# Query tiles loaded twice from DRAM and scaled while scores are copied, in a threshold-attention and mixture-of-attention kernel

## The chip, the cores and the metric

The kernel runs on one core of one Trainium2 chip. The metric is the device time of one execution in microseconds (us). Three executions of the kernel before took 933.61, 934.09 and 937.35 us; their median, 934.09 us, is the time before. TensorE is called PE here (its weight loads PEld), VectorE DVE, ScalarE ACT, GpSimd POOL, and the engine that only issues transfers SP.

## The reference, cut to what matters

Eight batches, eight heads, 576 positions, head size 64. The first part is an attention whose scores below the row's maximum minus `tau` are dropped; its output, with heads side by side, is the input of the second part, four causal attentions ("experts") of which a gate takes the best two at each position.

```python
scale = 1.0 / np.sqrt(q.shape[-1])                     # 1/8
scores = scale * np.matmul(q, k.transpose(0, 1, 3, 2))
thresh = np.max(scores, axis=-1, keepdims=True) - tau
scores = np.where(scores >= thresh, scores, -1000000000.0)
attn = np.exp(scores - np.max(scores, axis=-1, keepdims=True))
attn = attn / (np.sum(attn, axis=-1, keepdims=True) + 1e-09)
x = np.matmul(attn, v)                                 # then (8, 576, 512)
logits = x @ w_gate                                    # best 2 of 4 experts
for e in range(4):
    q, k, v = x @ wq[e], x @ wk[e], x @ wv[e]
    a = softmax(causal(scale * (q @ k.transpose(0, 2, 1))))
    out += weight[e] * (a @ v @ wo[e])
```

## The kernel before, in words

**Tiling.** The first part works on 32 pairs of heads: pair n is batch n // 4 and heads 2 (n % 4) and the next. A head's 576 queries are four tiles of 128 rows and a tail of 64; the two tails of a pair make one tile. A score tile is 128 rows by 576 keys and fills two banks of PSUM. So a pair has nine score tiles, and the program 288. PE holds float32 operands as two parts, a rounded one (`hi`) and the rest (`lo`), and makes each product from three matmuls; much of it runs on one half of the array, two matmuls side by side.

**A pair, step by step.** `load(n)` (line 365) sends the transfers: eight of keys (`ki`), two of queries (`qi`), two of query tails (`qit`), three of values (`vm`, `vt`). `scale_q` and `scale_qt` (lines 871 to 875) multiply the queries by `qsc`, which is minus 1/8, and write them twice side by side (`qi2`, `qit2`): on POOL for every pair but the first, which has them on ACT and DVE. `prep(n)` (line 391) turns keys and queries round on PE, ACT writes the `hi` part (`kk`, `qq`, `qz`) and DVE the `lo` part. `scores` (line 408) then does, for each tile: the matmuls (`s_main`, line 932); `s_min` on DVE (line 945), which copies the scores out of PSUM with an addition of zero and keeps the row's minimum (the sign is turned, so that is the maximum's place); `s_thr`, the threshold; `s_exp` on ACT (line 960); `s_stt`, the mask (line 962), a DVE instruction that reads scores and exponentials from SBUF, compares, multiplies and sums; `tr_pp`, transposes of the result on PE (profile line 826); and `out_t`, their copy to SBUF on ACT (line 812, out of `ps` into `pt`). `attnv` (line 448) sums the row sums, inverts them, spreads them with POOL into `iw` (lines 977 to 983), transposes them on PE and multiplies by `v` (`av`).

**The second part**, `second(b)` (line 515), projects the whole batch with PE, evacuates each result with an ACT copy and a DVE addition, runs the gate, scores, exponentials, POOL scaling (`p`, line 1225), transposes, products and output. It starts when the four pairs of a batch are done and is mixed with the pairs of the next batch. The last batch's second part has no pairs beside it.

**What sets the order.** The kernel makes a list of tasks, and `plan` (line 155) runs an event simulation over them when the program is built: each task has a length per engine, a priority, buffers that it takes (`SLOTS`) and tasks that it waits for. An idle engine takes the ready task of least priority. The priorities are sums of the table `PR`, the rates `PJ`, `VJ`, `S2J`, `TAILK`, and some hundreds of numbers in `TUNE`. Engines then execute their own lists strictly in the order planned. Until `COLD`, PE fills its gaps with matmuls on a constant tile (`ones`).

**Queues.** Transfers are issued by SP or by ACT; an issue stands in the engine's list with its other work. `load` sets `e = "SP" if n else "ACT"` for the queries, and so they are planned. The transfers are lambdas that read `e` when they are called, and line 380 has set `e` to "POOL" or "DVE" by then; `dma` (line 838) sends everything that is not "SP" to ACT. Thus all 128 query transfers are issued by ACT, at the places where the plan had SP issue them. Transfers of both queues take turns on eight completion semaphores, `DMAHW0` to `DMAHW7`; an issue that takes one of them again waits until the transfer that had it before is complete.

Of the kernel before, what the change touches and what calls it, by code (L numbers as in the profile page):

```python
# [11 lines left out]
F32 = mybir.dt.float32  # L12
# [72 lines left out]
class Space:  # L85
# [8 lines left out]
    def pick(self, cls, now, taken, kept):  # L94
        ok = [self.banks[i] <= now and i not in taken and i not in kept and (i != IDLE or now >= COLD) for i in range(8)]
        if cls == "s":
            pairs = [i for i in range(0, 6 if now <= EARLY else SHI, 2) if ok[i] and ok[i + 1]]
            return pairs[0] if pairs and sum(ok) - 2 >= LEAVE else None
        if cls == "d":
            pairs = [i for i in range(DLOW, 8, 2) if ok[i] and ok[i + 1]]  # L100
            return pairs[-1] if pairs else None
# [53 lines left out]
def plan(tasks, filler=None):  # L155
# [9 lines left out]
    moved = 0.0  # L165
# [11 lines left out]
    def begin(e, now):  # L177
        best, full, kept = None, set(), set()
        for pri, _, t in ready[e]:
# [3 lines left out]
            if e == "PE":  # L183
# [4 lines left out]
                if best is not None and p >= best[0]:  # L188
                    continue
# [13 lines left out]
    while events:  # L203
# [23 lines left out]
        for e in engines:  # L227
# [24 lines left out]
            at[e], t.end = start + occ, start + lat  # L252
# [11 lines left out]
def t_act(n):  # L264
    return 172 + 0.84 * n, 110
# [29 lines left out]
def work(K):  # L295
# [69 lines left out]
    def load(n):  # L365
        b, hp = divmod(n, NPAIR)
        pri = 5 * (n - 1) - 3.0 + PR["ld"]
        ki, qi, qit, qi2, qit2, vm = (Buf(x) for x in ("ki", "qi", "qit", "qi2", "qit2", "vm"))
# [3 lines left out]
        dq = [dma(lambda j=j: K.load_q(n, j, e), (), pri + 0.01, [qi], name=f"ldq.{n}", e=e) for j in range(2)]  # L372
        dt = [dma(lambda j=j: K.load_qt(n, j, e), (), pri + 0.01, [qit], move=72.0, name=f"ldq.{n}", e=e) for j in range(2)]
# [17 lines left out]
    def prep(n):  # L391
        ki, qi, qit, vm, dk, sq, st, dv = LD[n]
# [925 lines left out]
```

## Time and profile before

| | |
|---|---|
| median of three executions | 934.09 us |
| the profiled execution | 935.23 us, of which the span from the first to the last instruction 933.3 us |
| busy, share of the span | PE 95%, PEld 84%, DVE 79%, ACT 75%, POOL 46% |
| mean granted PE clock | 0.995 of full speed |

A share of busy time is a mean over the whole span. An engine that is not busy was waiting for another, or it was issuing a transfer, which isn't counted as busy. The chain of waits starts at the last instruction and goes back, at each step to what released it; it says which engine's work was last at each moment, and its shares add up to the span. PE can be busy with other work while the chain runs over ACT or DVE.

### The profile page before, as it was taken

How to read it: one execution, taken by the hardware profiler on the slowest of the kernel's cores; microseconds unless marked ns; L12 is line 12 of the kernel's file. 1: busy time of each engine (PE TensorE's matmuls, PEld its weight loads, DVE VectorE, ACT ScalarE, POOL GpSimd, SP SyncE). 2: the span in 40 equal slices, each digit the busy share in tenths (PEclk: the TensorE clock that was granted, in tenths of full speed). 3: DMA queues.
4: the chain of work that ended last, by engine and by line, in shares of the span. 5: the costliest groups of instructions: out<-in, count | busy, mean ns of one | idle time of the engine just before them, and what ended most of it. 6: DMA issues, size and time to landing. Idle time of an engine off the chain costs nothing.

```text
span 933.3 us, 36267 instructions
## 1 busy us (share of the span) xinstructions
PE 882.3 (95%) x14809; PEld 785.9 (84%) x14809; DVE 740.0 (79%) x2114; ACT 700.8 (75%) x1491; POOL 428.7 (46%) x724
## 2 busy tenths in 40 slices
PE   9888999999999999989999899998999999999997
PEld 7777898889887998879888798877988789887996
DVE  5899898777888768896888968798787977888554
ACT  5888869776787767887777876887677886778546
POOL 4654344632644436345265433644335533453373
PEclk9999999999999999999999999999999999999999
DMA  3433111120111202112111211112021121110001
GB/s 78 103 82 73 32 39 41 40 63 25 40 41 40 63 21 56 41 40 51 31 50 36 59 45 53 36 34 69 17 61 42 42 59 27 40 26 2 25 25 58
DMA packets 131030, 42.21 MB, mean 45 GB/s; under 512 B 126000, under 2 KB 126000, under 8 KB 130864
## 3 DMA queue, kind: packets, MB, share of 16 engines
q1 hardware_dynamic: 91808, 30.44, 12.9%
q10 hardware_dynamic: 39056, 9.45, 4.6%
q8 instruction: 117, 1.92, 0.9%
q14 instruction: 49, 0.40, 0.1%
HBM read 30.42 MB, written 9.44 MB: 43 GB/s over the span
## 4 chain that ended last, share of the span: by engine, by line
PE 58%; DVE 16%; ACT 10%; POOL 6%; issue 5%; DMA 3%; ACTq 1%; POOLq 0%; DVEq 0%
PE ps L836 46%; PE ps L826 12%; DVE e L964 6%; ACT pt L812 5%; DVE sc L947 4%; DMA vm<-in_v_dram 3%; ACT e L960 2%; POOL p L1225 2%; ACT p L1205 2%; DVE sm L1198 1%; ACTq L839 1%; POOL q2d L816 1%; POOL k L820 1%; DVE iv L1027 1%; DVE qq L820 1%
## 5 line engine op out<-in xcount | busy, mean ns | idle before, releaser
L812 ACT ACTIVATE pt<-ps 128x640 f32<-128x640 f32 (+3 forms) x400 | 251.6, 661 | 50.7 <-PE ps L826 43.2
L964 DVE SCALAR_TENSOR_TENSOR e<-sc,sm,e 128x576 f32<-128x576 f32 x288 | 250.3, 884 | 28.0 <-ACT e L960 24.6
L960 ACT ACTIVATE e<-sc,sm 128x576 f32<-128x576 f32 x288 | 220.7, 774 | 52.1 <-DVE sc L947 32.6
L947 DVE TENSOR_SCALAR_CACHE_REDUCE sc<-ps 128x576 f32<-128x576 f32 x288 | 215.2, 751 | 47.0 <-PE ps L836 42.8
L836 PE MATMUL ps<-kk,qq 64*128 64x288 f32 x1536 | 173.9, 325 | 6.0 <-ACT pt L812 3.1
L836 PE MATMUL ps<-pt,vm 128*64 128x128 f32 (+1 forms) x2560 | 159.9, 267 | 0.2
L826 PE MATMUL ps<-ident,e 64*128 64x64 f32 x2880 | 139.5, 228 | 13.7 <-ACT pt L812 4.6
L1225 POOL TENSOR_SCALAR p<-p,sm,gw 128x384 f32<-128x384 f32 (+4 forms) x144 | 100.9, 708 | 108.3 <-ACT pt L812 34.2
L826 PEld LDWEIGHTS ps<-ident,e 64*128 64x128 f32 x2880 | 118.6, 139 | 29.9 <-ACT pt L812 9.9
L836 PEld LDWEIGHTS ps<-pt,vm 128*64 128x64 f32 x2560 | 128.8, 137 | 11.9 <-issue 4.2
L836 PEld LDWEIGHTS ps<-kk,qq 64*128 64x128 f32 x1536 | 119.7, 191 | 20.1 <-ACT pt L812 7.2
L836 PE MATMUL ps<-x,wh 64*128 64x288 f32 x1024 | 105.0, 294 | 0.0
L816 POOL TENSOR_SCALAR iw<-sg 128x256 f32<-128x256 f32 (+1 forms) x96 | 44.5, 475 | 101.7 <-DVE sg L972 64.2
L836 PEld LDWEIGHTS ps<-x,wh 64*128 64x128 f32 x1024 | 87.3, 185 | 0.5 <-ACT pt L812 0.3
L836 PE MATMUL ps<-x,wl 64*128 64x288 f32 x512 | 81.5, 292 | 0.0
L812 ACT ACTIVATE iv<-ps 128x288 f32<-128x288 f32 (+2 forms) x128 | 53.0, 422 | 34.5 <-PE ps L836 19.5
L1205 ACT ACTIVATE p<-ps,sm 128x512 f32<-128x512 f32 (+3 forms) x128 | 67.2, 531 | 10.2 <-DVE sm L1198 9.7
L836 PE MATMUL ps<-pt,v 128*64 128x128 f32 (+1 forms) x960 | 60.9, 264 | 7.1 <-DVE sc L947 3.9
L836 PE MATMUL ps<-wh,x 64*128 64x260 f32 x640 | 66.2, 286 | 0.0
L869 POOL TENSOR_SCALAR qi<-qi,qsc 128x1024 f32<-128x1024 f32 x31 | 38.0, 1224 | 52.6 <-PE ps L826 50.8
L836 PE MATMUL ps<-pt,vt 128*64 128x128 f32 (+1 forms) x640 | 59.1, 262 | 0.0
L836 PEld LDWEIGHTS ps<-pt,v 128*64 128x64 f32 x960 | 45.3, 138 | 15.9 <-DVE sc L947 6.8
(124 smaller groups left out, 1631.0 us busy)
## 6 DMA issues: line engine op xcount, KB each, us to landing
ki<-in_k_dram SPq DMA_DIRECT2D x256, 36.0 KB, 1.9
qi<-in_q_dram ACTq DMA_DIRECT2D x64, 128.0 KB, 2.7
vm<-in_v_dram SPq DMA_DIRECT2D x64, 128.0 KB, 2.6
out_dram<-ob SPq DMA_DIRECT2D x32, 256.0 KB, 2.1
qit<-in_q_dram ACTq DMA_DIRECT2D x64, 16.0 KB, 2.0
vt<-in_v_dram SPq DMA_DIRECT2D x32, 32.0 KB, 2.4
out_dram<-ob SPq DMA_DIRECT2D x8, 128.0 KB, 2.4
ob<-in_moe_wq_dram SPq DMA_DIRECT2D x4, 128.0 KB, 2.4
```

The source lines that it names most:

```text
L812: self.nc.scalar.activation(dst, src, AF.Copy)
L816: self.nc.gpsimd.tensor_scalar(dst, src, 1.0, 0.0, op0=ALU.mult, op1=ALU.add)
L820: eng.tensor_tensor(dst, a, b.bitcast(F32), op=ALU.subtract)
L826: self.nc.tensor.transpose(self.ps[:, bank, c * n:(c + 1) * n], x[sl], self.ident[sl, sl])
L836: self.nc.tensor.matmul(out, x, y, start=first, stop=last)
L839: (self.nc.sync if e == "SP" else self.nc.scalar).dma_start(dst, src)
L869: (self.nc.vector if e == "DVE" else self.nc.gpsimd).tensor_scalar(out, t, self.qsc, 0.0, op0=ALU.mult, op1=ALU.add)
L947: self.nc.vector.tensor_scalar(self.sides(sc), self.dbank(s)[:, :, :HS], 0.0, None, op0=ALU.add, op1=ALU.min, accum_out=self.small(sm)[:, ...
L960: self.nc.scalar.activation(self.row(e), self.row(sc), AF.Exp, bias=self.small(sm)[:, 2 * j:2 * j + 1], scale=-1.0)
L964: self.nc.vector.scalar_tensor_tensor(self.row(e), self.row(sc), self.small(sm)[:, 8 + j:9 + j], self.row(e), op0=ALU.is_le, op1=ALU.mult, ...
L1205: self.nc.scalar.activation(self.p2(p2)[:, j * SM:j * SM + w], self.dbank(g)[:, j, :w], AF.Exp, bias=m[:, 2 * j:2 * j + 1], accum_out=m[:, ...
L1225: self.nc.gpsimd.tensor_scalar(p, p, self.small(sm)[:, 10 + j:11 + j], g[:, o:o + 1], op0=ALU.mult, op1=ALU.mult)
```

## The change

Queries go straight into `qi2` and `qit2`: each transfer is sent twice, once for each of the two copies. The scaling steps are gone; `s_min` multiplies by `qsc` in the place where it added zero. The buffers `qi` and `qit` fall away, `e` gets a sixth and `q2d` a second buffer. The lambdas now read an `e` that isn't set again, so pairs 1 to 31 issue their queries from SP and pair 0 from ACT. `plan` learns that the mask waits for POOL and POOL for the mask (`port`); pairs of PSUM banks may start at an odd number (`ODD`); the spreading of `iw` may go to POOL or ACT (`IWE`). The lengths that `plan` takes for `s_min`, `s_exp`, `s_stt` and ACT's small step, six constants, the tile order of the first batch (`TS0`) and every number of `TUNE` are new.

```diff
-    "qi": 1, "ki": 1, "qit": 1, "qi2": 1, "qit2": 1, "vm": 2, "kk": 2, "qq": 2, "qz": 2, "sc": 4, "e": 5, "sg": 3, "iw": 1, "iv": 3, "pt": 8,
-    "x0": 2, "x1": 2, "x2": 1, "x3": 1, "sm": 8, "q2": 2, "k2": 2, "q2d": 1, "p2": 3, "v2": 2,
+    "ki": 1, "qi2": 1, "qit2": 1, "vm": 2, "kk": 2, "qq": 2, "qz": 2, "sc": 4, "e": 6, "sg": 3, "iw": 1, "iv": 3, "pt": 8,
+    "x0": 2, "x1": 2, "x2": 1, "x3": 1, "sm": 8, "q2": 2, "k2": 2, "q2d": 2, "p2": 3, "v2": 2,
...
+            elif t.port:
+                p += SHY * max(0.0, at["POOL"] - now - 200.0)
...
-            at[e], t.end = start + occ, start + lat
+            more = 0.0
+            if t.port:
+                more = max(0.0, at["POOL"] - start - 200.0)
+                port = start + more + 640.0
+            elif e == "POOL":
+                more = max(0.0, port - start)
+            at[e], t.end = start + occ + more, start + lat + more
...
-        dq = [dma(lambda j=j: K.load_q(n, j, e), (), pri + 0.01, [qi], name=f"ldq.{n}", e=e) for j in range(2)]
-        dt = [dma(lambda j=j: K.load_qt(n, j, e), (), pri + 0.01, [qit], move=72.0, name=f"ldq.{n}", e=e) for j in range(2)]
+        dq = [dma(lambda j=j, x=x: K.load_q(n, j, x, e), (), pri + 0.01, [qi2], name=f"ldq.{n}", e=e) for j in range(2) for x in range(2)]
+        dt = [dma(lambda j=j, x=x: K.load_qt(n, j, x, e), (), pri + 0.01, [qit2], move=72.0, name=f"ldq.{n}", e=e) for j in range(2) for x in range(2)]
...
-        e = "POOL" if n else "DVE"
-        st = task(e, (270, 30), lambda: K.scale_qt(e), dt, 5 * (n - 1) - 1, [qit2], [qit], name=f"qs.{n}")
-        e2 = "POOL" if n else "ACT"
-        sq = task(e2, (1200, 30) if n else t_act(2 * SM), lambda: K.scale_q(e2), dq, 5 * (n - 1) - 1, [qi2], [qi], name=f"qs.{n}")
-        LD[n] = (ki, qi2, qit2, vm, dk, sq, st, dv)
+        LD[n] = (ki, qi2, qit2, vm, dk, dq, dt, dv)
...
-            m = task("DVE", (825, 75), lambda j=j: K.s_min(bufs[j], scs[j], sm, j), [a], i + PR["max"], [],
+            m = task("DVE", (747, 75), lambda j=j: K.s_min(bufs[j], scs[j], sm, j), [a], i + PR["max"], [],
...
-        u = [task("POOL", t_pool(nm * P), lambda: K.g_wide(sg, iw, nm), [r], i + PR["nrm"], [iw], [sg, iw], name=f"iw.{n}.{first}")]
+        u = [evac(nm * P, lambda e: K.g_wide(e, sg, iw, nm), [r], i + PR["nrm"], [iw], [sg, iw], name=f"iw.{n}.{first}", engs=IWE)]
...
+IWE = ('POOL', 'ACT')
...
-W_FROM = 23858.152
-W_EACH = 2325.47
+W_FROM = 19276.174
+W_EACH = 6514.406
...
-        self.nc.vector.tensor_scalar(self.sides(sc), self.dbank(s)[:, :, :HS], 0.0, None, op0=ALU.add, op1=ALU.min,
+        self.nc.vector.tensor_scalar(self.sides(sc), self.dbank(s)[:, :, :HS], self.qsc, None, op0=ALU.mult, op1=ALU.min,
```

**Where it moves instructions.** On ACT, in the middle of the program, at the place where pair 20's queries have been turned and pair 22's are sent for. Before (`qq`, `pt`, `e`, `p` are the tiles of the steps above):

```order
L812 ACTIVATE qq_838_10378<-ps 128x512
L812 ACTIVATE pt_840_10417<-ps 128x640
L839 DMA qi<-in_q_dram 128x4x64 x2
L812 ACTIVATE pt_842_10439<-ps 128x512
L960 ACTIVATE e_844_10462<-sc_841_10429,sm_83 128x576
L812 ACTIVATE pt_845_10475<-ps 128x640
L812 ACTIVATE pt_846_10486<-ps 128x640
L812 ACTIVATE pt_848_10493<-ps 128x512
L839 DMA qit<-in_q_dram 64x64
L960 ACTIVATE e_849_10502<-sc_843_10449,sm_83 128x576
L839 DMA qit<-in_q_dram 64x64
```

The same place of ACT's list now:

```order
L828 ACTIVATE qq_837_10398<-ps 128x512
L828 ACTIVATE pt_839_10439<-ps 128x640
L828 ACTIVATE pt_840_10461<-ps 128x512
L828 ACTIVATE pt_841_10481<-ps 128x512
L828 ACTIVATE pt_842_10494<-ps 128x640
L828 ACTIVATE pt_844_10506<-ps 128x640
L963 ACTIVATE e_846_10527<-sc_843_10496,sm_81 128x576
```

The four issues are gone from between the copies; behind the opening, ACT's list has no transfer. The copies stand in nearly the order they had.

On SP, a little over one round of four pairs, in the middle of the program. Before (`ki` keys, `vm` and `vt` values, `ob` results going out):

```order
L839 DMA ki<-in_k_dram 48x3x64 x16
L839 DMA vm_110<-in_v_dram 128x4x64 x2
L839 DMA vt_113<-in_v_dram 64x2x64
L839 DMA ki<-in_k_dram 48x3x64 x8
L839 DMA vm_109<-in_v_dram 128x4x64 x2
L839 DMA vt_111<-in_v_dram 64x2x64
L839 DMA ki<-in_k_dram 48x3x64 x8
L839 DMA out_dram<-ob_687_8479 128x512
```

SP in the matching round now (`qi_72` and `qit_73` are the doubled buffers `qi2` and `qit2`):

```order
L855 DMA qit_73<-in_q_dram 64x64 x4
L855 DMA ki<-in_k_dram 48x3x64 x10
L855 DMA qi_72<-in_q_dram 128x4x64 x4
L855 DMA vm_108<-in_v_dram 128x4x64 x2
L855 DMA vt_111<-in_v_dram 64x2x64
L855 DMA qit_73<-in_q_dram 64x64 x4
L855 DMA qi_72<-in_q_dram 128x4x64 x4
L855 DMA ki<-in_k_dram 48x3x64 x8
L855 DMA out_dram<-ob_689_8538 128x512
```

Where a pair had 11 loads in SP's list it has 19, and the eight of the queries stand between those of the keys and the values.

At the opening of the program, on ACT. Before:

```order
L839 DMA qi<-in_q_dram 128x4x64 x2
L839 DMA qit<-in_q_dram 64x64 x2
L779 ACT_TABLE_LOAD
L779 ACTIVATE warm<-eps 128x2
L867 ACTIVATE qi_74<-qi,qsc 128x1024
L812 ACTIVATE qq_1_243<-ps 128x512 x2
```

And now:

```order
L855 DMA qi_72<-in_q_dram 128x4x64 x4
L855 DMA qit_73<-in_q_dram 64x64 x4
L828 ACT_TABLE_LOAD
L828 ACTIVATE qq_1_232<-ps 128x512
L795 ACTIVATE warm<-eps 128x2
```

Eight issues stand ahead of ACT's first instruction where there were four, and the scaling between them and `qq` is gone.

## Rows read from the trace of the kernel before

**Rows 1.** The page's first part: busy us of each engine (share of the span) x instructions.

```profile
span 933.3 us, 36267 instructions
...
PE 882.3 (95%) x14809; PEld 785.9 (84%) x14809; DVE 740.0 (79%) x2114; ACT 700.8 (75%) x1491; POOL 428.7 (46%) x724
```

**Rows 2.** Busy time in stretches of the span: the first batch of pairs, one of the middle rounds, the end; then ten-microsecond pieces of the first batch. Columns: from:to, length, busy us (x instructions) of each engine, granted PE clock, DMA share, GB/s.

```profile
0.00:128.50 128.50, 116.61 (x1847) 102.11 (x1849) 106.05 (x293) 96.79 (x177) 64.36 (x143) 0.99 0.31 69
466.90:580.00 113.10, 108.12 (x1850) 96.99 (x1848) 92.00 (x267) 86.67 (x185) 51.49 (x80) 1.00 0.19 45
868.00:933.40 65.40, 59.84 (x914) 52.80 (x910) 30.17 (x85) 36.66 (x107) 30.00 (x55) 0.99 0.11 38
40.00:50.00 10.00, 8.72 (x148) 7.37 (x148) 9.95 (x28) 9.03 (x17) 7.29 (x9) 1.00 0.48 107
50.00:60.00 10.00, 8.72 (x162) 7.22 (x156) 9.90 (x25) 8.83 (x19) 5.28 (x7) 1.00 0.45 107
```

**Rows 3.** The page's fourth part, the chain that ended last, its shares of the span by engine and by line.

```profile
PE 58%; DVE 16%; ACT 10%; POOL 6%; issue 5%; DMA 3%; ACTq 1%; POOLq 0%; DVEq 0%
PE ps L836 46%; PE ps L826 12%; DVE e L964 6%; ACT pt L812 5%; DVE sc L947 4%; DMA vm<-in_v_dram 3%; ACT e L960 2%; POOL p L1225 2%; ACT p L1205 2%; DVE sm L1198 1%; ACTq L839 1%; POOL q2d L816 1%; POOL k L820 1%; DVE iv L1027 1%; DVE qq L820 1%
```

**Rows 4.** The timeline around ACT's issues for the next pair, in the place of the first order above: start, length, engine, line, operation, and in brackets the idle time before and what ended it.

```profile
517.84 0.94 SPq L839 DMA_DIRECT2D vm<-in_v_dram  x2
518.02 1.12 POOL L869 TENSOR_SCALAR qi<-qi,qsc 128x1024 f32<-128x1024 f32 x1
...
518.72 0.71 ACT L812 ACTIVATE pt<-ps 128x640 f32<-128x640 f32 x1 [0.64 <-PE ps L826]
...
519.17 1.12 ACTq L839 DMA_DIRECT2D qi<-in_q_dram  x2
...
520.40 0.60 ACT L812 ACTIVATE pt<-ps 128x512 f32<-128x512 f32 x1 [0.97 <-DMA vm<-in_v_dram]
...
521.05 0.53 PE L826 MATMUL ps<-ident,e 64*128 64x64 f32 x10 [0.59 <-ACT pt L812]
...
522.31 0.28 PE L826 MATMUL ps<-ident,qit 64*128 64x64 f32 x2 [0.28 <-ACT pt L812]
...
522.90 0.66 PE L836 MATMUL ps<-kk,qq 64*128 64x288 f32 x6 [0.32 <-ACT pt L812]
```

**Rows 5.** The transfers' line: issues on each queue, and their length in ns, least, median and most.

```profile
L839 SPq DMA_DIRECT2D ki<-in_k_dram x256: 311/427/1835, 0.8 to 819.0; - x128
L839 ACTq DMA_DIRECT2D qi<-in_q_dram x64: 369/375/1301, 1.3 to 758.5; - x64
L839 ACTq DMA_DIRECT2D qit<-in_q_dram x64: 472/483/1317, 2.3 to 770.1; - x64
L839 SPq DMA_DIRECT2D vm<-in_v_dram x64: 372/455/1348, 5.7 to 835.5; - x64
L839 SPq DMA_DIRECT2D vt<-in_v_dram x32: 607/610/1664, 6.8 to 836.1; - x32
```

**Rows 6.** The longest waits of PE, summed over the span: who, for whom, us in total, times, longest.

```profile
PE ps L826 <- ACT pt L812: 7.7, 17, 0.7
PE ps L836 <- ACT pt L812: 6.0, 21, 0.6
PE ps L826 <- POOL iw L816: 5.7, 7, 1.1
```

**Rows 7.** Groups of POOL by shape: busy us, mean ns | idle before, releasers.

```profile
L869 POOL TENSOR_SCALAR qi<-qi,qsc 128x1024 f32<-128x1024 f32 x31 | 38.0, 1224 | 52.6 <-PE ps L826 50.8 <-DMA qi<-in_q_dram 1.8
...
L869 POOL TENSOR_SCALAR qit<-qit,qsc 128x128 f32<-128x128 f32 x31 | 15.9, 514 | 64.1 <-PE ps L826 42.1 <-DMA qit<-in_q_dram 12.0 <-DVE sm L1000 10.0
L816 POOL TENSOR_SCALAR iw<-sg 128x128 f32<-128x128 f32 x32 | 15.5, 485 | 0.0
```

**Rows 8.** The mask and the score copy: groups of DVE by shape, and the mask's lengths in ns (least, median, most).

```profile
L964 DVE SCALAR_TENSOR_TENSOR e<-sc,sm,e 128x576 f32<-128x576 f32 x288 | 250.3, 884 | 28.0 <-ACT e L960 24.6 <-ACT sm L955 1.4
L947 DVE TENSOR_SCALAR_CACHE_REDUCE sc<-ps 128x576 f32<-128x576 f32 x288 | 215.2, 751 | 47.0 <-PE ps L836 42.8 <-ACT pt L812 2.7
...
L964 DVE SCALAR_TENSOR_TENSOR e<-sc,sm,e x288: 773/817/1586, 16.9 to 866.8; 128x576 f32<-128x576 f32 x144
```

**Rows 9.** The opening, on ACT and PE.

```profile
2.30 1.50 ACTq L839 DMA_DIRECT2D qit<-in_q_dram  x2
3.83 1.28 ACT L779 ACT_TABLE_LOAD   x1 [3.83 <-DMA ki<-in_k_dram]
...
5.28 1.15 ACT L867 ACTIVATE qi<-qi,qsc 128x1024 f32<-128x1024 f32 x1
7.30 1.08 ACT L812 ACTIVATE qq<-ps 128x512 fp32r<-128x512 f32 x2 [0.87 <-PE ps L826]
...
12.05 0.60 PE L836 MATMUL ps<-kk,qq 64*128 64x288 f32 x1
```

**Rows 10.** DMA: the page's third part for the queue of the loads, the landing of queries, and the shortest round of the key buffer, from its release by PE to its next use.

```profile
q1 hardware_dynamic: 91808, 30.44, 12.9%
...
qi<-in_q_dram ACTq DMA_DIRECT2D x64, 128.0 KB, 2.7
...
588.91 0.60 PE L826 MATMUL ps<-ident,ki 48*128 48x48 f32 x11
599.44 0.69 PE L826 MATMUL ps<-ident,ki 48*128 48x48 f32 x12
```

More of the change, by code (lines that the diff above doesn't have):

```diff
@@ L66, in __init__ @@
         self.move = 0.0
+        self.port = False
         self.takes = takes
@@ L96, in pick @@
         if cls == "s":
-            pairs = [i for i in range(0, 6 if now <= EARLY else SHI, 2) if ok[i] and ok[i + 1]]
+            hi = 6 if now <= EARLY else SHI
+            pairs = [i for k in range(1 + ODD) for i in range(k, hi - k, 2) if ok[i] and ok[i + 1]]
             return pairs[0] if pairs and sum(ok) - 2 >= LEAVE else None
         if cls == "d":
-            pairs = [i for i in range(DLOW, 8, 2) if ok[i] and ok[i + 1]]
-            return pairs[-1] if pairs else None
+            pairs = [i for k in range(1 + ODD) for i in range(6 - k, DLOW - 1, -2) if ok[i] and ok[i + 1]]
+            return pairs[0] if pairs else None
         one = [i for i in range(GLOW, 8) if ok[i]]
@@ L164, in plan @@
     mode = None
-    moved = 0.0
+    moved = port = 0.0
     order = []
@@ L187, in begin @@
                     p += BACK * space.scores
[L188 to L189 removed]
+            elif t.port:
+                p += SHY * max(0.0, at["POOL"] - now - 200.0)
+            if best is not None and p >= best[0]:
+                continue
             new = [b for b in t.takes if b.slot is None]
@@ L341, in small @@
     def small(engs, fn, deps, pri, sm, name):
-        x = task(None, {e: (200, 30) if e == "POOL" else SMALL for e in engs}, None, deps, pri, [], [sm], name=name)
+        x = task(None, {e: (200, 30) if e == "POOL" else (290, 110) if e == "ACT" else SMALL for e in engs}, None, deps, pri, [], [sm], name=name)
         x.fn = lambda: fn(x.by)
@@ L367, in load @@
         pri = 5 * (n - 1) - 3.0 + PR["ld"]
-        ki, qi, qit, qi2, qit2, vm = (Buf(x) for x in ("ki", "qi", "qit", "qi2", "qit2", "vm"))
+        ki, qi2, qit2, vm = (Buf(x) for x in ("ki", "qi2", "qit2", "vm"))
         e = "SP" if n else "ACT"
@@ L472, in attnv @@
         a = None
-        for s in order:
+        if AVM:
+            a = pe(sum(10 * (109.2 if s < R else 58.4) for s in order),
+                   lambda: [K.av(g, (s - first) * P, vm, PTS[n, s][0], s) for s in order],
+                   [*LD[n][7], *[y for s in order for y in PTS[n, s][1]]], i + PR["av"], [g, x],
+                   [vm, *[y for s in order for y in PTS[n, s][0]]], "C", 53.0, name=f"av.{n}.{first}")
+        for s in order if not AVM else ():
             pts, c = PTS[n, s]
@@ L861, in load_vt @@
         self.dma(self.vts[vm.slot][ST:], self.v[b, 2 * hp:2 * hp + 2, SM:, :].rearrange("h s d -> s h d"))
-    def scaled(self, e, out, t):
-        t = t.unsqueeze(2).to_broadcast(out.shape)
-        if e == "ACT":
-            self.nc.scalar.activation(out, t, AF.Copy, scale=self.qsc)
-        else:
-            (self.nc.vector if e == "DVE" else self.nc.gpsimd).tensor_scalar(out, t, self.qsc, 0.0, op0=ALU.mult, op1=ALU.add)
-    def scale_qt(self, e):
-        self.scaled(e, self.qit2.unsqueeze(1), self.qit.unsqueeze(1))
-    def scale_q(self, e):
-        self.scaled(e, self.qi2, self.qi.rearrange("p r j d -> p (r j) d"))
     def tr_k(self, g):
```

54 lines of the change are left out of this document (29 added, 25 removed).

## The prediction

> **What bounds the kernel now.** I read the busy shares first: PE is at work for 882.3 of 933.3 us, so it idles for 51.0 us, and no other engine passes 79% [rows 1]. Then the stretches. The first batch of pairs idles PE for 128.5 - 116.6 = 11.9 us, a middle round for 113.1 - 108.1 = 5.0 us, the end for 65.4 - 59.8 = 5.6 us [rows 2]. In the first batch DVE is the bound for a while: 9.95 and 9.90 of 10 us between 40 and 60 us, while PE has 8.7 [rows 2]. The granted clock is 0.99 or more of the 2.4 GHz level in all these stretches, so the clock is not the matter.
>
> Next the chain. PE has only 58% of it; DVE has 16%, ACT 10%, POOL 6%, and 3% stands under a DMA whose line is that of the values, 1% under ACT's sequencer at line 839, a transfer's issue [rows 3]. No copy on ACT reads values from DRAM. What this means is seen in the timeline around 519 us [rows 4]: ACT has to issue two query loads; the first needs the scaled tile's source buffer, on which POOL works from 518.02 to 519.14, and the other takes a completion semaphore that SP's value loads, issued from 517.84, had before. The next copy starts at 520.40, after 0.97 us without work, and PE then waits 0.59, 0.28 and 0.32 us for ACT's copies. So a query load on ACT holds the copies queued behind it, and PE behind them. The issue alone is 375 ns for `qi` and 483 ns for `qit`, 64 of each [rows 5]: 64 x 0.375 + 64 x 0.483 = 54.9 us of ACT's list.
>
> **The change part by part.** The sum is made against the profiled execution: 935.2 us, that is 933.3 of span and 1.9 around it, 1.1 above the median.
>
> *Query loads leave ACT.* 120 of 128 issues go, near 120 x 0.43 = 52 us of ACT's list, with the waits in front of them. From above, the end moves by all that the chain has under "DMA" and "ACTq", 3% + 1% of 933 or 37 us [rows 3]; from below by nothing, if PE's queue hides it. What PE shows is nearer the low end: its waits for ACT's copies are 7.7 + 6.0 = 13.7 us [rows 6], and the one place looked at gives 0.59 + 0.28 + 0.32 = 1.2 us [rows 4]. I take 1.2 us there and 0.3 us at the other three pairs of a round together, for seven rounds: 1.5 x 7 = 10 us. What is late next there is the score copy on DVE and the exponential behind it, which have 4% and 2% of the chain. Against this, 36 of the 96 `iw` steps now stand in ACT's list; this trace has none on ACT, so I bound one from POOL's 485 ns for it [rows 7]: at most 17 us, a third of what ACT gets back.
>
> *The scaling leaves POOL.* 38.0 + 15.9 = 53.9 us of 428.7 [rows 1, 7]. POOL idles for more than half of the span, so this counts only where PE waits for POOL: 5.7 us for `iw`, in seven places [rows 6]. I take 3 us, between 0 and 5.7; DVE's row sums, from which `iw` is made, are late next.
>
> *The mask and the port.* The mask takes 884 ns in the mean, 817 in the median [rows 8]. So 288 x 0.067 = 19 us of DVE go to some long ones. POOL loses 54 of 429 us, an eighth, and the plan now sees the collision. DVE counts only where it is the bound, about a third of the first batch: I take 1 us, between 0 and 19 x 128.5 / 933 = 2.7. The Trainium skill, "SBUF — State Buffer", section "Who interferes with whom", says that a VectorE instruction with two SBUF inputs and a GpSimd instruction that reads SBUF lock each other out for the whole of an instruction. That fits long masks beside short ones in these rows. By that rule alone an estimate with random meetings would give 38.0 / 933 of the 288 masks, 12 of them, half a scaling step each, 7 us of DVE in the whole span; the sum above would get 1 us more.
>
> *The score copy multiplies.* Same engine, same shape, 288 times at 751 ns [rows 8]. The mask also reads a column of numbers per partition and costs 66 ns more with two inputs from SBUF, so the ends are 0 and 288 x 0.066 = 19 us of DVE. Nearest is the copy itself, which only changes its operation: 0.
>
> *The opening.* Eight issues stand ahead of ACT's table load where four did. Two `qit` took 1.50 us together with the waits for semaphores, and the table load started at 3.83 us [rows 9]. Four more at 0.4 to 0.75 us put it at 5.5 to 6.8; with its 1.28 us the first `qq` copy can start at 6.8 to 8.1, against 7.30. The last `qit` lands 2 to 2.7 us after its issue, near 9, and PE's list has the tails' transposes ahead of the keys', so the first score matmul comes at 12 to 14 us against 12.05. I take 1 us later, between 1 earlier (the 1.15 us of scaling are gone) and 2 later.
>
> *Twice the query bytes, on one queue.* 64 x 512 packets more for the tiles, and 4096 for the tails, 36,864 on top of 91,808 that took 12.9% of the DMA engines' time [rows 10]: 5% more, hidden by engines that are idle for over 80% of a middle round [rows 2]. SP's list has per pair 8 x 0.427 + 4 x 0.375 + 4 x 0.483 + 2 x 0.455 + 0.607 = 8.4 us of issues [rows 5] against 28 us that a pair takes, a quarter of a round [rows 2]. The cover is smallest where a key buffer is free at 589.5 and wanted again at 599.4 us [rows 10]: up to sixteen issues, 6.9 us, and 2.7 us to land are 9.6 of 9.9 us. I take 0, between 0 and 16 (2 us in each of eight rounds).
>
> *The new order.* Row counts and the sequence of copies in ACT's list are close to those before, so I give it 0, between 10 us lost and 10 won, a fifth of PE's idle time each way.
>
> Sum: - 10 - 3 - 1 + 0 + 1 + 0 + 0 = - 13 us. 935.2 - 13 = 922.2 for a profiled execution, and 1.1 less, **921 us**, as a median.
>
> **The rivals.** *PE has it hidden already.* The bound is 95% busy and its idle time has many small causes; each hold that goes uncovers the next wait, here DVE's. For it: DVE's chain share of 16% is larger than ACT's. Against it: the hold at 519 us is of ACT's own making. It would give 932 to 936, say 934 us.
>
> *Late loads.* Before, queries had a landing buffer of their own and could be two pairs ahead; now each load waits until PE has turned the pair before, and 19 loads stand in one list with the results' stores. If an issue waits for such a store, or a semaphore, for 0.7 us past the 0.3 us of cover that I find, keys and queries are late for that pair. It decides from the point where sixteen issues and a landing exceed 9.9 us; at 0.7 us in each of 31 pairs it costs 22 us, and the end is at 921 + 22 = 943 us, slower than before. For it: single key loads have taken up to 1.8 us to issue [rows 5]. Against it: SP is idle for most of a round, and the plan now counts these loads where they stand.
>
> *More than the idle time.* Weight loads are at work for 785.9 us, 84% [rows 1], and PE has only 58% of the chain [rows 3], so a matmul marked busy can be one that waits. The Trainium skill, "Perfetto Trace Analysis", section "Identifying the Most-Contended Engine", says that the busy share of matmuls measures badly how near TensorE is to its limit, and the busy share of weight loads better. In numbers of this kernel: if the chain's 37 us for DMA and ACT's sequencer go wholly, with 3 us of POOL, less 11 us that `iw` and the opening take, the end is at 934 - 29 = 905 us.
>
> **How the numbers follow.** The forecast, 912 to 929 us, has 0.56; more than the idle time 0.18; hidden already 0.14; late loads, or an order that is worse by itself, 0.12. About 0.5%, 4.7 us, is what a measurement of this kernel can tell from no change. Forecast and third rival are faster, 0.74; the first rival is the same, 0.14; the second slower, 0.12. The range reaches down to the third rival's 905 and up to 938, where it takes in the first rival and the smaller half of the second's prices; I leave some 0.08 below and 0.08 above.
>
> **What would show it.** In the page of the changed kernel no query load stands under ACT's queue except eight, and the lines "DMA" and "ACTq" of the chain fall from 4% to under 1%. PE's waits for `pt` copies fall from 13.7 to under 8 us, those for `iw` from 5.7 to under 3. POOL's busy time falls to near 360 us, the mask's mean to 840 to 870 ns, and a middle round lasts about 111 us. The score copy stays at 751 ns. I am wrong if ACT's waits shrink and the rounds stay at 113 us (hidden), if PE's transposes of keys or queries wait for a DMA (late loads), or if the score copy grows past 770 ns.

## The result: 906.25 us, 3.1% faster

Run beside each other, the kernel before took 935.43 us (median, 933.61 to 937.35) and the changed one 906.25 us (905.23 to 906.58): a ratio of 0.969, interval 0.966 to 0.971, or 29.2 us less. The forecast was 13 us less. The time is inside the predicted range, at its low end, and next to what the rival "more than the idle time" gives. The experiments below show that neither the forecast's terms nor that rival's mechanism made most of it: 19.5 of the 29 us came with the new order and what was planned along with it, and the prediction had put the order at 0. That the time lies in the range and near that rival is chance.

**The profile after.** The changed kernel's page, busy us of each engine (answering [rows 1]):

```profile
span 904.6 us, 36394 instructions
...
PE 877.8 (97%) x14813; PEld 786.4 (87%) x14813; DVE 732.3 (81%) x2106; ACT 705.5 (78%) x1533; POOL 355.4 (39%) x627
```

PE idles 904.6 - 877.8 = 26.8 us, where it idled 51.0. That is 24.2 us; the other 4.5 us of the span's 28.7 came out of PE's *busy* time, for the same matmuls. So busy time was no floor. POOL has lost 73.3 us: 53.9 are the scaling, and most of the rest are the `iw` steps that ACT has now.

Stretches of the changed kernel's span: the first batch, a middle round and the end (columns as in [rows 2]):

```profile
0.00:124.70 124.70, 113.75 (x1785) 98.87 (x1787) 103.55 (x285) 94.10 (x178) 52.04 (x128) 0.97 0.40 88
311.20:418.50 107.30, 105.93 (x1838) 95.72 (x1836) 90.30 (x264) 86.97 (x191) 41.52 (x67) 1.00 0.24 56
839.20:904.60 65.40, 60.38 (x904) 52.93 (x900) 29.70 (x85) 35.37 (x103) 28.59 (x53) 0.99 0.11 38
```

A middle round takes 107.3 us instead of 113.1, and PE idles 1.4 us of it instead of 5.0. The first batch is 3.8 us shorter, of which 0.9 are idle time (11.0 us instead of 11.9), at a granted clock of 0.97 against 0.99; the end is as long as it was. So most of the gain is in the middle.

What PE waits for in the changed kernel (us in total, times, longest; answering [rows 6]):

```profile
PE ps L842 <- DVE e L967: 3.5, 3, 2.3
PE ps L842 <- DVE sc L950: 2.4, 7, 0.8
PE ps L852 <- ACT pt L828: 2.2, 8, 0.5
...
PE ps L842 <- ACT pt L828: 0.9, 1, 0.9
...
PE ps L842 <- ACT iw L828: 0.3, 2, 0.2
```

The waits for `pt` copies are 2.2 + 0.9 = 3.1 us (13.7 before), those for `iw` 0.3 (5.7 before), and none that is listed is for a DMA. Groups by shape, for the mask and the copy (answering [rows 8]):

```profile
L967 DVE SCALAR_TENSOR_TENSOR e<-sc,sm,e 128x576 f32<-128x576 f32 x288 | 236.6, 834 | 9.1 <-ACT e L963 6.7 <-ACT sm L958 0.4
L950 DVE TENSOR_SCALAR_CACHE_REDUCE sc<-ps,qsc 128x576 f32<-128x576 f32 x288 | 232.2, 811 | 45.3 <-PE ps L852 32.5 <-PE ps L842 5.8 <-issue 3.3
```

The mask is 50 ns shorter (884 to 834), 14.4 us of DVE in all. The score copy is 60 ns *longer* (751 to 811), 17.3 us, which the prediction put at 0. Transfers: SP issues 124 of each kind of query load, ACT the eight of the opening; the queues of SP (q1) and of ACT (q10), answering [rows 5, 10]:

```profile
L855 SPq DMA_DIRECT2D qi<-in_q_dram x124: 366/497/1589, 8.8 to 774.5; - x124
L855 SPq DMA_DIRECT2D qit<-in_q_dram x124: 465/587/1774, 11.3 to 789.9; - x124
```

```profile
q1 hardware_dynamic: 167200, 48.74, 22.5%
...
q10 hardware_dynamic: 2576, 0.59, 0.3%
```

The chain of the changed kernel's profile breaks off after about a fifth of the span, so its shares can't be set beside [rows 3].

### The profile page after: what moved, and what is told of

It reads as the page before. It is cut to its first block, busy times and chain, and to the rows that moved or that the text cites. A ratio compares the mean times of both kernels' runs of the same rounds, so it can differ in the third digit from the quotient of the medians.

```text
span 904.6 us, 36394 instructions
## 1 busy us (share of the span) xinstructions
PE 877.8 (97%) x14813; PEld 786.4 (87%) x14813; DVE 732.3 (81%) x2106; ACT 705.5 (78%) x1533; POOL 355.4 (39%) x627
## 5 line engine op out<-in xcount | busy, mean ns | idle before, releaser
L950 DVE TENSOR_SCALAR_CACHE_REDUCE sc<-ps,qsc 128x576 f32<-128x576 f32 x288 | 232.2, 811 | 45.3 <-PE ps L852 32.5
L967 DVE SCALAR_TENSOR_TENSOR e<-sc,sm,e 128x576 f32<-128x576 f32 x288 | 236.6, 834 | 9.1 <-ACT e L963 6.7
L852 PE MATMUL ps<-kk,qq 64*128 64x288 f32 x1536 | 169.3, 321 | 2.8 <-DVE sc L950 1.2
L1228 POOL TENSOR_SCALAR p<-p,sm,gw 128x512 f32<-128x512 f32 (+4 forms) x144 | 101.4, 713 | 164.2 <-ACT pt L828 63.8
L842 PEld LDWEIGHTS ps<-ident,e 64*128 64x128 f32 x2880 | 122.8, 139 | 22.9 <-ACT pt L828 5.8
L852 PEld LDWEIGHTS ps<-kk,qq 64*128 64x128 f32 x1536 | 118.9, 189 | 14.4 <-DVE sc L950 3.3
L832 POOL TENSOR_SCALAR x<-iv 128x320 fp32r<-128x320 f32 (+1 forms) x64 | 37.1, 579 | 119.7 <-DVE iv L1030 61.7
L1208 ACT ACTIVATE p<-ps,sm 128x384 f32<-128x384 f32 (+3 forms) x128 | 66.3, 524 | 9.2 <-DVE sm L1201 4.2
L832 POOL TENSOR_SCALAR iw<-sg 128x256 f32<-128x256 f32 (+1 forms) x60 | 25.5, 429 | 120.7 <-DVE sg L975 65.6
L1201 DVE TENSOR_REDUCE sm<-ps 128x2 f32<-128x1024 f32 (+3 forms) x64 | 52.4, 819 | 8.6 <-PE ps L852 8.4
L852 PE MATMUL ps<-pt,v 128*64 128x128 f32 (+1 forms) x960 | 57.9, 260 | 0.2 <-DVE ob L1108 0.2
```

Of the source, the lines that this page charges most:

```text
L832: self.nc.gpsimd.tensor_scalar(dst, src, 1.0, 0.0, op0=ALU.mult, op1=ALU.add)
L842: self.nc.tensor.transpose(self.ps[:, bank, c * n:(c + 1) * n], x[sl], self.ident[sl, sl])
L852: self.nc.tensor.matmul(out, x, y, start=first, stop=last)
L950: self.nc.vector.tensor_scalar(self.sides(sc), self.dbank(s)[:, :, :HS], self.qsc, None, op0=ALU.mult, op1=ALU.min, accum_out=self.small(s ...
L967: self.nc.vector.scalar_tensor_tensor(self.row(e), self.row(sc), self.small(sm)[:, 8 + j:9 + j], self.row(e), op0=ALU.is_le, op1=ALU.mult, ...
L1201: self.nc.vector.tensor_reduce(self.small(sm)[:, :3:2], self.dbank(g)[:, :, :w], axis=AX.X, op=ALU.max, negate=True)
```

## The experiments

Times are medians; the kernel before took 935.2 to 935.6 us beside these runs. Single executions of one version lie 1 to 6 us apart, so a difference of two medians is known to about 2 us. Three theories: A, ACT's list was held by issues and their waits; B, POOL's scaling and the port; C, the new order. A first group takes before's own order and puts one part after another into it.

**Query loads on SP, in the old order.** `e` is no longer set again, so the loads' lambdas read "SP"; nothing else changes.

```diff
-        e = "POOL" if n else "DVE"
-        st = task(e, (270, 30), lambda: K.scale_qt(e), dt, 5 * (n - 1) - 1, [qit2], [qit], name=f"qs.{n}")
+        e1 = "POOL" if n else "DVE"
+        st = task(e1, (270, 30), lambda: K.scale_qt(e1), dt, 5 * (n - 1) - 1, [qit2], [qit], name=f"qs.{n}")
```

> The kernel before, with its 124 query transfers of pairs 1 to 31 issued by SP instead of ACT; every engine's order is otherwise the one before, POOL still scales. Theory A (ACT's list was held by the issues and their waits, and that is most of the gain of 29 us): 910 to 920 us, PE's waits for the pt copies fall from 13.7 to under 6 us. Theory B (the gain is the scaling that leaves POOL, and the port): 930 to 936 us. Theory C (the gain is the new order of the plan): 928 to 936 us.

Measured: 927.28 us (925.48 to 929.15), ratio 0.992 (0.990 to 0.994): 8 us less, too little for theory A and a little more than B or C alone would give. PE's waits for `pt` fall from 13.7 to 4.9 + 3.2 = 8.1 us; those for `iw` stay at 5.7.

```profile
PE ps L836 <- ACT pt L812: 4.9, 15, 0.7
...
PE ps L826 <- ACT pt L812: 3.2, 7, 0.6
```

The page's chain of this run:

```profile
PE 59%; DVE 20%; ACT 8%; issue 6%; POOL 5%; DMA 1%; POOLq 0%; ACTq 0%; SPq 0%; DVEq 0%
```

DMA and ACTq have gone from 4% to 1%, some 28 us of chain, and 8 us came off the time: DVE has 20% where it had 16%. What a chain holds at one place is not what its removal gives, because the next chain is only a little shorter.

**The same without POOL's scaling.** `scaled` does nothing when its engine is POOL, so this version leaves out the scaling, and the turning of queries no longer waits for their loads; the changed kernel does wait for them.

```diff
-        else:
+        elif e != "POOL":
             (self.nc.vector if e == "DVE" else self.nc.gpsimd).tensor_scalar(out, t, self.qsc, 0.0, op0=ALU.mult, op1=ALU.add)
```

> Leaves out part of the computation: POOL's scaling of the queries of pairs 1 to 31, so that all pairs use pair 0's scaled queries. Otherwise as the run before with query loads on SP (927.3 us), in the order of before; POOL's list loses 54 us (62 steps) and nothing else changes. Theory B, POOL's length decides: PE's 5.7 us of waits for iw fall under 2 us, the mask goes from 883 to about 850 ns, and the time falls by more than 8 us, to 910 to 919 us. Theory C, the new order is what remains: by waits for iw and for DVE's mask alone at most 5 us come off, 922 to 927 us, and the other 15 to 20 us down to the changed kernel are the order's. In between: both.

Measured: 923.42 us (922.76 to 924.27), ratio 0.9875 (0.986 to 0.989): 3.9 us less than the run before it, as theory C expected, but not where it expected it. The mask goes from 883 to 870 ns only. Of PE's waits, those at line 826 for the `lo` part of the queries (`qq`) fall from 2.6 to 0.6 us, and the 0.8 us for `q2d` and some smaller ones go; how much of this is POOL's time and how much the missing wait for the loads, the run does not part. The waits for `iw` did not move:

```profile
PE ps L826 <- POOL iw L816: 5.6, 6, 1.0
```

Five of these six are 1.0 us each, at the same place in five rounds. The timeline of one:

```profile
474.08 0.18 DVE L972 RECIPROCAL sg<-sg 128x4 f32<-128x4 f32 x1
...
474.56 1.24 POOL L816 TENSOR_SCALAR q2d<-q 64x128 fp32r<-64x128 f32 x2
...
475.87 0.41 POOL L816 TENSOR_SCALAR iw<-sg 128x256 f32<-128x256 f32 x1
...
476.33 0.34 PE L826 MATMUL ps<-ident,iw 64*128 64x64 f32 x4 [1.04 <-POOL iw L816]
```

DVE's inverse is ready at 474.26. POOL is on the second part's `q2d` until 475.80 and starts `iw` after it. No scaling is near: the wait is made by the order of POOL's list.

**The same, with `iw` earlier in POOL's list.** The planned order stays, but each `iw` step is put right behind the DVE step that it needs (and behind the last transposes `ti`, which read the old `iw`). 25 of the 96 steps move past a POOL step, all but one past just one.

```diff
+def early_iw(order):
+    out = []
+    for t in order:
+        name = t.name or ""
+        if name.startswith("iw."):
+            key = name[3:]
+            at = max(i for i, x in enumerate(out) if (x.name or "") in ("inv." + key, "iw." + key) or (x.name or "").startswith("ti.")) + 1
+            out.insert(at, t)
+        else:
+            out.append(t)
+    return out
...
-        for t in plan(work(em), em.fill):
+        for t in early_iw(plan(work(em), em.fill)):
```

> As the run with loads on SP and without POOL's scaling (923.4 us; it leaves out the scaling of pairs 1 to 31), in the order of before, but each iw step stands in POOL's list right behind the DVE step that it needs, ahead of a POOL step or two (once in each round q2d) that stood before it. If PE's waits for iw, 5.6 us of which 5 are the same 1.0 us in five rounds, are made by the order of POOL's list: they fall under 2 us and the time by 3 to 5 us, to 918 to 920 us. If POOL's being busy in general, or DVE's late sums, made them: the waits stay over 4 us and the time within 2 us of 923.

Measured: 918.69 us (918.32 to 919.06), ratio 0.982 (0.979 to 0.985): 4.7 us less. The waits for `iw` are 0.4 us. The same place in this run:

```profile
472.49 0.18 DVE L972 RECIPROCAL sg<-sg 128x4 f32<-128x4 f32 x1
...
472.96 0.29 POOL L816 TENSOR_SCALAR q2d<-q 64x128 fp32r<-64x128 f32 x1
...
473.22 0.40 POOL L816 TENSOR_SCALAR iw<-sg 128x256 f32<-128x256 f32 x1
...
473.67 0.34 PE L826 MATMUL ps<-ident,iw 64*128 64x64 f32 x4
473.70 0.68 POOL L816 TENSOR_SCALAR q2d<-q 64x128 fp32r<-64x128 f32 x1
```

`iw` now stands between the two halves of `q2d`, and PE no longer waits. Twenty-five such moves in POOL's list, five of them past `q2d`, are worth as much as the removal of 54 us of POOL work.

**The column, in the old order.** Without scaling as above (`iw` where the plan had it), and `s_min` multiplies by `qsc`.

```diff
-        self.nc.vector.tensor_scalar(self.sides(sc), self.dbank(s)[:, :, :HS], 0.0, None, op0=ALU.add, op1=ALU.min,
+        self.nc.vector.tensor_scalar(self.sides(sc), self.dbank(s)[:, :, :HS], self.qsc, None, op0=ALU.mult, op1=ALU.min,
```

> As the run without scaling, and the score copy multiplies by the column qsc where it added zero, in the order of before; the scores of it are scaled once too often. If the column costs 60 ns per copy in any order, DVE's copy goes from 751 to about 811 ns, DVE's busy time rises by 17 us, and the time rises by about 7 us, as between the changed kernel and its version with a number. If before's order hides it, it rises by less than 3 us; if before's order, planned with 825 ns for the copy but less cover for DVE, shows more of it, by 10 us or more. The distance from here to the changed kernel's 906 us is then what the new order, with the doubled loads and iw on two engines, gives.

Measured: 925.76 us (923.53 to 927.02), ratio 0.990 (0.988 to 0.992); 2.3 us more than without the column, hardly outside the scatter. Every edit of the change is now in, in the old order, but for the second copy of each load, pair 0's new opening, ACT's share of `iw`, the buffers and the odd banks. The distance to the changed kernel is 925.76 - 906.25 = 19.5 us. Page, a middle round, PE's waits and two groups of this run:

```profile
PE 884.3 (96%) x14809; PEld 786.0 (85%) x14809; DVE 745.6 (81%) x2114; ACT 699.1 (76%) x1491; POOL 376.4 (41%) x662
```

```profile
522.40:632.90 110.50, 107.36 (x1832) 95.82 (x1828) 91.48 (x264) 85.83 (x183) 44.20 (x72) 1.00 0.19 47
```

```profile
PE ps L836 <- ACT pt L812: 4.5, 15, 0.7
PE ps L826 <- POOL iw L816: 4.4, 6, 0.8
PE ps L836 <- DVE sc L947: 3.8, 14, 0.6
PE ps L826 <- DVE sc L947: 3.6, 10, 0.7
PE ps L826 <- ACT pt L812: 2.8, 6, 0.6
```

```profile
L964 DVE SCALAR_TENSOR_TENSOR e<-sc,sm,e 128x576 f32<-128x576 f32 x288 | 243.4, 861 | 21.9 <-ACT e L960 18.6 <-ACT sm L955 0.2
L947 DVE TENSOR_SCALAR_CACHE_REDUCE sc<-ps,qsc 128x576 f32<-128x576 f32 x288 | 232.1, 811 | 42.3 <-PE ps L836 39.3 <-issue 1.2 <-ACT sm L955 0.6
```

From here to the changed kernel PE's idle time goes from 38.5 to 26.8 us and its busy time from 884.3 to 877.8, together the 18.2 us of the two spans. The score matmuls alone have 5.3 us of the busy time: 174.6 to 169.3 us for the same 1536, with a median of 293 and 292 ns, so it is the long ones that became shorter. Of the waits, `iw` gives back 4.4 - 0.3 = 4.1 us, `pt` 7.3 - 3.1 = 4.2, the score copy 7.4 - 4.0 = 3.4 (the changed kernel has 2.4 and 1.6). The column costs 811 ns in either order; the mask is 861 ns here and 834 in the new order.

A second group takes the changed kernel and puts one part back.

**All query loads on ACT, in the new order.** The calls get "ACT" in the place of `e`.

```diff
-        dq = [dma(lambda j=j, x=x: K.load_q(n, j, x, e), (), pri + 0.01, [qi2], name=f"ldq.{n}", e=e) for j in range(2) for x in range(2)]
+        dq = [dma(lambda j=j, x=x: K.load_q(n, j, x, "ACT"), (), pri + 0.01, [qi2], name=f"ldq.{n}", e=e) for j in range(2) for x in range(2)]
```

> The changed kernel, with all query transfers issued by ACT again, at the places where SP issued them; no engine's compute order changes. Eight issues a pair, 0.37 to 0.48 us each, 31 x 8 x 0.43 = 107 us of ACT's list. Theory A: 925 us or more. Theories B and C: under 915 us.

Measured: 920.45 us (919.77 to 922.52), ratio 0.985 (0.983 to 0.987): 14.2 us more than the changed kernel, with twice the issues that the old order had. This lies between what A and what B and C expected. PE's waits for ACT come back, among them

```profile
PE ps L852 <- ACT pt L828: 4.3, 13, 0.6
...
PE ps L842 <- ACT pt L828: 3.1, 9, 0.9
PE ps L852 <- ACT iv L828: 2.8, 2, 1.5
```

Theory A is real in both orders: 8 of 29 us in the old one, and 14 in the new one, where it has twice the issues to hold.

**POOL work put back, in two doses.** `tr_q` gets small POOL steps on a scratch tile for which nothing waits: six per pair, then three.

```diff
+    def again(self):
+        for i in range(6):
+            self.nc.gpsimd.tensor_scalar(self.scr, self.scr, self.qsc, 0.0, op0=ALU.mult, op1=ALU.add)
...
     def tr_q(self, g, j):
+        if j:
+            self.again()
```

> The changed kernel with six added POOL steps per pair on a scratch tile of 128 x 80, on which nothing waits, at the place where the pair's queries are turned: about 1.5 to 1.8 us of POOL a pair, as much as the scaling took. Theory B (POOL's length and the port carry a good part of the gain): 912 us or more, and the mask's mean grows from 834 to 860 ns or more. Theories A and C: 905 to 909 us.

> The changed kernel with three small POOL steps per pair on a scratch tile where the run before had six (931.7 us with 78 us of POOL work, 25 us slower). About 39 us of POOL work, somewhat under the 54 us that the scaling took. If each us of POOL costs the same: 12 us slower, 918 us. If the new order has some room on POOL and only the excess is paid: 3 us or less, 909 us, with waits of PE for iw and p under 4 us together.

Measured: six steps, 931.69 us (929.61 to 934.57), ratio 0.996 (0.995 to 0.998), 25 us slower than the changed kernel; three steps, 909.49 us (909.26 to 910.7), ratio 0.973 (0.971 to 0.974), 3.2 us slower. The groups of these steps and PE's largest waits, first with six:

```profile
L891 POOL TENSOR_SCALAR scr<-scr,qsc 128x80 f32<-128x80 f32 x192 | 78.2, 407 | 15.3
```

```profile
PE ps L844 <- POOL iw L834: 12.3, 8, 2.1
PE ps L844 <- POOL p L1238: 9.5, 8, 1.5
```

and with three:

```profile
L891 POOL TENSOR_SCALAR scr<-scr,qsc 128x80 f32<-128x80 f32 x96 | 38.9, 405 | 6.3
```

```profile
PE ps L844 <- ACT iw L830: 2.8, 6, 0.5
...
PE ps L844 <- POOL iw L834: 1.9, 6, 0.3
...
PE ps L844 <- POOL p L1238: 1.8, 7, 0.4
```

Six steps were 78.2 / 32 = 2.4 us a pair, more than was meant. The first 39 us cost 3, the next 39 cost 22. POOL has a cover, and past it PE waits; with three steps the waits for `iw` and `p` are already 6.5 us, not under 4. (With six steps the mean granted clock was 0.985 against 0.995. Of the 27.3 us that the span grew, 19.5 are idle time of PE and 7.8 busy time; a slower clock would lengthen the busy time.) The mask hardly took part: 845 ns with three steps and 848 with six against 834. The scaling's 54 us lie between the doses; if the cost only grows with the dose, they would have cost the new order something between 3 and 25 us, and they cost the old one 3.9 at most.

**All `iw` steps on POOL.** `g_wide` and `g_tail` name "POOL" in the place of `e`; the order is the changed kernel's.

> The changed kernel with its order, but all 96 iw steps on POOL (36 of them stood on ACT). ACT loses 13 us, POOL gains about 15 us, at places where PE waits for the result. If POOL's length at these places is what decides: PE waits again for POOL's iw, 3 to 6 us, and the time is 909 to 914 us. If the steps stood on ACT only for balance: within 2 us of 906.

Measured: 906.09 us (905.36 to 907.11), ratio 0.969 (0.967 to 0.970), the same as the changed kernel. PE's waits for `iw` do not come back. So in this order they stay away because of where the steps stand, not because ACT takes 36 of the 96.

**The score copy by a number.** The column holds minus 1/8 wherever `tau` is not negative; here the instruction holds that number.

```diff
-        self.nc.vector.tensor_scalar(self.sides(sc), self.dbank(s)[:, :, :HS], self.qsc, None, op0=ALU.mult, op1=ALU.min,
+        self.nc.vector.tensor_scalar(self.sides(sc), self.dbank(s)[:, :, :HS], -SCALE, None, op0=ALU.mult, op1=ALU.min,
```

> The changed kernel, with the score copy multiplying by a constant in the instruction (-1/8) instead of a column of numbers per partition; for tau of 0 or more, as here, the two are the same number. The copy's mean goes from 811 back to 751 ns. If DVE's length counts in the end (17 us of DVE): 897 to 903 us. If PE hides it: 904 to 907 us.

Measured: 898.97 us (897.37 to 899.18), ratio 0.961 (0.960 to 0.963): 7.3 us less than the changed kernel, and the best version here. The group of the copy and the page's busy line and chain:

```profile
L950 DVE TENSOR_SCALAR_CACHE_REDUCE sc<-ps 128x576 f32<-128x576 f32 x288 | 215.8, 752 | 47.5 <-PE ps L852 33.6 <-PE ps L842 5.8 <-issue 2.8
```

```profile
PE 873.6 (97%) x14813; PEld 784.0 (87%) x14813; DVE 719.0 (80%) x2106; ACT 703.2 (78%) x1533; POOL 354.2 (39%) x627
...
PE 72%; DVE 17%; ACT 5%; issue 4%; POOL 1%; DMA 1%; SPq 0%; DVEq 0%; ACTq 0%; POOLq 0%
```

The copy is back at 752 ns: the multiplication is free, the column is not. 4.2 of the 7.1 us of span come out of PE's busy time. The chain, which can be read here, has 72% on PE against 58% in [rows 3].

**The old numbers in the new planner.** The changed kernel with its rules, lengths and loads, but `TUNE`, the rates, `TS0`, `W_FROM`, `W_EACH` and `EARLY` of before; then the same with `iw` on POOL alone, even banks only and five `e` buffers.

```diff
-IWE = ('POOL', 'ACT')
+IWE = ('POOL',)
...
-ODD = 1
+ODD = 0
```

> The changed kernel with everything it knows (port, lengths, doubled loads on SP, iw on POOL or ACT, six buffers of e), but the fitted numbers of before (TUNE, the rates, TS0, W_FROM, W_EACH, EARLY), so that its order is another one. If what the planner knows gives the gain of the order, this run is near the changed kernel, 906 to 915 us. If the gain of the order, 20 us, is that of numbers fitted to it, the run is at 930 us or more, no better than the order of before with the same parts (925.8 us).

> As the run with the old fitted numbers, and the three new freedoms taken back (iw on POOL alone, bank pairs start at even numbers, five buffers of e), so that these numbers meet the choices that they were fitted to; of the planner's news the port and the lengths are left. If knowing the port and the lengths is worth something by itself: below 922 us, and the mask at 840 ns or less against 861 in the order of before. If it is worth nothing without fitted numbers: 925 us or more.

Measured: 965.77 us (964.66 to 967.7), ratio 1.033 (1.029 to 1.036), and 943.5 us (941.6 to 944.59), ratio 1.008 (1.005 to 1.011). Both are slower than the kernel before, though all direct edits are in. The first one's page:

```profile
PE 909.0 (94%) x14809; PEld 800.8 (83%) x14809; DVE 749.2 (78%) x2108; ACT 709.5 (74%) x1534; POOL 344.6 (36%) x624
```

Its mean granted clock was 0.979, which by estimate is 909 x (0.995 - 0.979) = 15 us of the 60 to the changed kernel. Its mask takes 862 ns, the second run's 861, as in the old order, although the rule on the port is in both. What the planner knows is worth nothing here without numbers fitted to it. The old numbers were fitted to the old lengths and loads, so these runs say what a bad fit costs, not what each rule gives with a good one.

**The opening.** The version by a number, with ACT's table load ahead of the four `qit` issues.

```diff
+        warm = next(t for t in order if t.name == "warm")
+        fifth = [t for t in order if t.name == "ldq.0"][4]
+        order.remove(warm)
+        order.insert(order.index(fifth), warm)
```

> The version with a number in place of the column (899.0 us), and in the opening ACT's small first exponential, with which the table is loaded, stands between pair 0's four qi loads and its four qit loads, where it stood behind all eight and behind the first qq copy. In the changed kernel the table load started at 7.32 us, behind the wait for the qit issues, and the first qq copy at 8.62. If the opening's lateness (first score matmul at 13.62 us against 12.05 before) comes from the table load: qq starts at 7.5 to 8 us, the first score matmul near 13 us, and the time falls by up to 1 us. If the transposes of the tails behind the qit loads set it (they started at 9.99 us, and the loads are now issued no earlier): the first score matmul stays at 13.5 us or later and the time is the same.

Measured: 899.22 us (897.51 to 899.82), no change. ACT in the opening and the first score matmul, in the changed kernel, then ACT in this run:

```profile
4.71 2.58 ACTq L855 DMA_DIRECT2D qit<-in_q_dram  x4
7.32 1.28 ACT L828 ACT_TABLE_LOAD   x1 [7.32 <-DMA qit<-in_q_dram]
8.62 0.60 ACT L828 ACTIVATE qq<-ps 128x512 fp32r<-128x512 f32 x1
...
13.62 0.60 PE L852 MATMUL ps<-kk,qq 64*128 64x288 f32 x1
```

```profile
3.71 1.28 ACT L795 ACT_TABLE_LOAD   x1 [3.71 <-DMA ki<-in_k_dram]
...
5.50 3.09 ACTq L855 DMA_DIRECT2D qit<-in_q_dram  x4
8.64 1.08 ACT L828 ACTIVATE qq<-ps 128x512 fp32r<-128x512 f32 x2 [3.43 <-DMA qit<-in_q_dram]
```

The table load moves 3.6 us ahead and the first copy not at all: the four `qit` issues with their waits now end at 8.59 us, and the copy stands behind them. The first score matmul is at 13.90 us.

## Why the prediction was right or wrong

*Bound.* Right: PE, with the loss in many small waits of the middle rounds. Wrong was to take PE's busy time as fixed, which only the third rival doubted.

*Query loads leave ACT, - 10 us.* Right in kind and near in size: 8 us in the old order, 14 in the new with doubled loads. Waits for `pt` fell to 8.1 us by this step, the rest by the order.

*The scaling leaves POOL, - 3 us.* The size was near, 3.9 us at most, and partly by luck; the reason was wrong. The prediction expected it from PE's waits for `iw`, which stayed at 5.6 us; POOL's `q2d` ahead of `iw` made them, and the order took them away.

*The mask and the port, - 1 us.* The scaling's going shortens the mask by 13 ns, 883 to 870, which is 3.7 us of DVE and is inside the 3.9 us above. It is 861 once the column is in, and 834 in the new order. The traces show where the length sits, by whether a POOL step was running when a mask began. Before, the 136 masks that no POOL step overlaps took 814 ns in the mean and 821 at most; the 92 that began while a POOL step ran took 1027. With the column in the old order these are 160 masks at 814 and 74 at 983, in the changed kernel 170 at 812 and 71 at 912. The scaling's going took such masks from 96 to 83, 13 fewer, near the 12 that the prediction estimated, but 3.7 us of DVE and not 7. The new order hardly makes the meetings fewer but makes them shorter. The Trainium skill, "SBUF — State Buffer", section "Who interferes with whom", has a DVE instruction with two SBUF inputs and a GpSimd instruction that reads SBUF lock each other out on a shared port. The trace agrees: only masks beside a POOL step are long. What the shorter masks are worth in time was not tried by itself.

*The score copy multiplies, 0.* The step that failed in the other direction. "Nearest is the copy itself, which only changes its operation" overlooked that the operand changes too, from a number to a column. The upper end, 66 ns and 19 us of DVE, was nearly what happened: 60 ns and 17.3 us. It costs 2 us in the old order and 7.3 us in the new one; that less else is in the way there is a reading, not shown. A copy past 770 ns was one of the prediction's own signs of being wrong.

*The opening, + 1 us.* The first score matmul starts at 13.62 against 12.05 us: 1.6 later, inside the range. The first `qq` copy starts at 8.62, later than the 6.8 to 8.1 forecast, for the four `qit` issues end only at 7.29 and the table load follows. The tails' transposes do come first, but PE waits there for DVE's part of `qq` behind that copy, not for the last `qit` to land. The table load ahead of the `qit` issues brought nothing.

*Twice the bytes on one queue, 0.* No wait of PE for a DMA appears, so "late loads" did not happen. One reading was wrong: [rows 10] has SP's queue alone, not all loads; the query loads moved to it as well as doubled, so q1 grew by 75,392 packets where the prediction added 36,864. Both queues together grew by 38,912, from 17.5% to 22.8% of the DMA engines' time, so the 5% more was right.

*The new order, 0.* This is the step that failed, and it made the forecast of 13 us less than half of the 29.2. "Row counts and the sequence of copies in ACT's list are close to those before, so I give it 0, between 10 us lost and 10 won" fails in both halves. With every direct edit in the old order the time is 925.8 us, and 906.25 in the new. By parts: - 8.0 (loads) - 3.9 (scaling) + 2.3 (column) - 19.5 (order, with what was planned along with it) = - 29.1 us. The last term is what is left, so the second copy of each load and the later opening are in it too. Two orders that the same planner makes from the same tasks, with new and with old numbers, took 906 and 966 us. And 25 moves by a place or two in POOL's list were worth 4.7 us: such moves can't be seen in counts, nor in another engine's list. The bound "a fifth of PE's idle time" was no bound, since 6.5 of the 18.2 us of span came from PE's busy time.

*The rivals.* "Hidden already" and "late loads" did not occur. "More than the idle time" named 905 us, and its doubt of busy time holds: PE was busy for 871.6 to 909.0 us in runs with the same matmuls (18 us of this are the clock's by estimate, 909 x (0.999 - 0.979)), so the busy sum depends on the order; that a long matmul is one that waits is a reading. The Trainium skill, "Perfetto Trace Analysis", section "Identifying the Most-Contended Engine", calls matmul busy time no good measure of how near TensorE is to its limit, and the trace agrees. But its sum, the chain's 37 us for DMA and ACT's sequencer "wholly", is refuted: 28 of them went, and 8 us came.

*The signs.* The waits for `pt` (3.1 us) and `iw` (0.3) and POOL's busy time (355.4) came as named. The mask (834 ns) and the round (107.3 us) went further than named, which belongs to the order. The fall of the chain's "DMA" and "ACTq" can't be read in the changed kernel.

*Still open.* Of the order's 19.5 us, 4.1 us stand opposite the waits for `iw`, and the moves in POOL's list show that such waits can be had back in the old order. For the other 15 the traces show which waits became shorter, not which of the moves did it, nor what six `e` buffers or odd banks are worth with numbers fitted to them.

## What to carry to other kernels

Where a change brings a new order, put its direct edits into the old order one by one and run that; what is then left is the order's, and it can outweigh the rest. Price an idle engine's work by what stands in its list just ahead of a step that the bound waits for, not by its busy sum. For an operand that changes kind, take a row with that kind of operand, and if the value is a constant, write it as a number.

## What the runs showed of the hardware

A column of one number per partition as the scalar of the 128x576 copy out of PSUM makes it 811 ns instead of 751, in both orders, while a multiplication by a number takes 752. POOL's 128x80 steps took 405 to 407 ns in the mean. POOL's `p` of 128x576 took 1149 ns before and 998 in the changed kernel. A mask of 128x576 that no POOL step overlaps took 812 to 815 ns in the mean in twelve of these kernels; those that began while a POOL step ran took 895 to 1052.
